# A segment's output projection summed in two PSUM banks (384 and 128 columns), and residual rows assembled once with their batched part

## The chip, the cores and the metric

One core of a Trainium2 chip. The metric is the device time of one execution in microseconds (us); lower is better. The kernel before took 1000.96 us (median of 3 runs, 999.44 to 1001.57). Executions of one kernel agree within about 0.5%.

## The reference

A transformer block with memory, followed by a gMLP. Only the first part matters for this change. The 2048 rows are cut into 64 segments of 32 rows. Each segment is joined with 8 memory rows, goes through attention with 32 heads, and the first 8 output rows are the memory of the next segment. So the segments are a serial chain.

```python
for s in range(n_seg):                       # 64 segments
    xs = x[:, s*seg_len:(s+1)*seg_len, :]    # 32 rows
    h = concatenate([mem, xs], axis=1)       # 40 rows
    q, k, v = h @ Wq, h @ Wk, h @ Wv         # 32 heads of 128
    p = softmax(where(mask, q k^T * scale, -1e9))
    o = (p @ v) @ Wo                         # output projection
    mem = o[:, :M, :]                        # 8 memory rows: the next segment needs them
    outs.append(o[:, M:, :])                 # 32 residual rows
# then h = x + outs, h2 = h + gMLP(layernorm(h)): "the tail" below
```

## The kernel before

An emitter records every operation with the tokens that it reads and writes, and derives the semaphore waits; each engine then runs its own list in program order. This is how waits are put in front of an instruction:

```python
for d in op.waits:                 # one wait for each engine or DMA that is still owed
    if d.is_dma: eng.wait_ge(dma_sems[d.dma_sem], d.dma_val)
    else:        eng.wait_ge(sems[d.eng], d.sigval)
ins = op.fn(eng)
```

PSUM, the memory that TensorE writes its sums to, is declared as 8 banks of 512 float32 columns (`ps`). The parts that the change touches (cut):

```python
def PV_half(s, b):                        # value products of one half of the heads
    for g in range(4):
        for c in range(4): ...            # matmul(ps[:, PVB[c], ...], lhsT=V_sb, rhs=E_sb[..., main columns])
            # reads ("V", b), ("E", b); PVB = (0, 1, 6, 7)
    for c in range(4): ...                # matmul(..., lhsT=Vx, rhs=E_sb[..., extra columns])
            # reads ("Vx", xb), ("E", b); Vx comes by DMA

def Wo(cs, first, last):                  # output projection: 8 matmuls for each c, four at a time (32 columns of the array each)
    for k, c in enumerate(cs):
        for bg in range(8): ...           # matmul(ps[32*g:32*g+32, OB, :], lhsT=cTh[...], rhs=w_o[:, h, :])   512 columns, bank OB
def part_evac(s):                         # ScalarE copies bank OB to SBUF
    act(... out=part[:, s % 4, :], in_=ps[:, OB, :] ...)
def mem_out(s):                           # 16 small matmuls pick and transpose the memory rows, ScalarE copies them to hT
    ...

# one segment, in TensorE's order (cut)
for b in range(2):
    for mi in range(2): QK(s, b, mi); QK_evac(s, b, mi)
S_half(s, 0); sm_exp(0); V_half(s, 0); V_evac(0, "dve"); sm_sums(0); sm_ln(0)
S_half(s, 1); sm_exp(1); sm_rcp(0); V_half(s, 1, (0, 1)); sm_sums(1); sm_ln(1); sm_rcp(1); V_half(s, 1, (2, 3))
V_evac(1, "act"); sm_norm(0); sm_norm(1)
ev = gx.pour(16)                          # 16 filler matmuls, work for a later chunk of 16 segments
PV_half(s, 0); PV_half(s, 1); ...         # then four cT evacuations
if rb > 0: WoX_mm(rb - 1, j4)             # batched part of the rows of four earlier segments
Wo((0, 2), True, False); Wo((1, 3), False, True)
cTx_copy(s); part_evac(s)
late = gv.pour(VXN[i16])                  # fillers: units of 4 matmuls; VXN = 2 in segments 0-11, 4 in 12 and 13, of 16
if j4 == 2: xT(0, XB) ...                 # 4 transposes in every fourth segment; likewise in number 13
mem_out(s)
for f in late: f()                        # ScalarE copies of the fillers (Vs)
if rb > 0 and j4 == 3: WoX_evac(rb - 1)   # ScalarE copy to partx
if j4 == 3:                               # every fourth segment
    F_group(rb, XB); F_add(rb, XB)        # residual rows of the last four segments
    if rb >= 1: WoX_scatter(rb - 1, WXB); h_done(rb - 1, WXB)   # and the batched part, read from partx
```

## Time and profile before

| what | value | view |
|---|---|---|
| span of the profiled execution | 997.6 us | page |
| first segment's first matmul, last segment's first matmul | 55.92, 804.53 us | timeline |
| from one segment's first matmul to the next's, plain segment | 11.64 us | timeline |
| the same for every fourth segment from number 7 on | 12.84 us; 12.33 to 12.36 in six of the fourteen | timeline |
| numbers 13 and 29 | 12.06 us | timeline |
| tail, from the last segment's first matmul to the end | 193.1 us | timeline |

Segments are counted from 0. "Plain" means: no residual work and no collision of fillers.

The windows view gives, for a stretch of time, the busy time of each engine, the clock that TensorE was granted, and the DMA share. In the segments TensorE is busy 93% of the time, at full clock, yet the time is set by a chain of waits:

```profile
core 0: us, PE busy (x) PEld busy (x) DVE busy (x) ACT busy (x) POOL busy (x), PEclk, DMA share, GB/s
400.00:600.00 200.00, 185.68 (x4749) 93.49 (x4744) 100.07 (x236) 118.45 (x271) 21.42 (x51) 1.00 0.19 47
815.00:997.00 182.00, 173.41 (x846) 78.96 (x851) 83.77 (x150) 36.85 (x64) 16.48 (x36) 1.00 0.26 78
```

The timeline lists instructions by start time: start, duration, engine, line, operation, output and inputs, shapes, count, and in brackets how long the engine idled before it and who ended that. Here is the end of a segment of the kernel before (TensorE and ScalarE lines that matter):

```profile
505.46 1.91 PE L581 MATMUL f_ps<-f_arena,f_cT 128*32 128x512 bf16 x32
...
507.20 0.60 PE L401 MATMUL f_ps<-f_arena,f_hTe 128*32 128x512 bf16 x8
507.43 0.60 ACT L593 ACTIVATE f_part<-f_ps 128x512 bf16<-128x512 f32 x1 [1.69 <-PE f_ps L581]
...
508.08 0.27 PE L599 MATMUL f_ps<-f_G_sb,f_part 128*32 128x8 bf16 x16 [0.27 <-ACT f_part L593]
...
508.42 0.20 ACT L602 ACTIVATE f_hT<-f_ps 128x32 bf16<-128x32 f32 x1 [0.40 <-PE f_ps L599]
...
508.67 0.61 PE L438 MATMUL f_ps<-f_arena,f_hT 128*32 128x512 bf16 x8 [0.33 <-ACT f_hT L602]
```

The projection (L581) starts at 505.46, and its last result comes at 507.37. Only then can ScalarE copy all 512 columns (L593, 0.60 us), the memory rows be picked (L599), copied (L602), and the next segment begin (L438) at 508.67: 3.21 us after the start of the projection, of which TensorE fills 0.43 us with two units of fillers (L401).

Every fourth segment ends so:

```profile
148.72 0.60 ACT L593 ACTIVATE f_part<-f_ps 128x512 bf16<-128x512 f32 x1 [1.69 <-PE f_ps L581]
...
149.37 0.27 PE L599 MATMUL f_ps<-f_G_sb,f_part 128*32 128x8 bf16 x16 [0.27 <-ACT f_part L593]
...
149.48 0.39 PE L608 MATMUL f_ps<-f_part,f_F_sb 128*32 128x512 bf16 x4
...
149.80 0.59 ACT L408 ACTIVATE f_Vs<-f_ps 128x512 bf16<-128x512 f32 x1
...
150.28 0.61 ACT L628 ACTIVATE f_partx<-f_ps 128x512 bf16<-128x512 f32 x1
...
150.94 0.40 PE L633 MATMUL f_ps<-f_partx,f_Sc 128*32 128x512 bf16 x4 [1.07 <-ACT f_partx L628]
...
151.16 1.04 PE L438 MATMUL f_ps<-f_arena,f_hT 128*32 128x512 bf16 x16
```

The copy of the batched part (L628, partx) is queued on ScalarE behind the fillers' copy (L408). TensorE's next instruction in order, the scatter (L633), waits 1.07 us for it, and the next segment's first matmul (L438) stands behind the scatter, although it needs nothing from it.

### The profile page before, as it was taken

The page shows a single profiled execution, that of the slowest core. Times are in us where ns is not written, and L with a number is a line of the kernel's source. Part 1 is how long each engine was busy: PE and PEld are TensorE (multiplying, and loading weights), DVE is VectorE, ACT ScalarE, POOL GpSimd, SP SyncE. Part 2 cuts the span into 40 slices and gives each one's busy share as a digit, 9 for nine tenths or more (in the row PEclk, how much of TensorE's full clock was granted, in tenths as well). Part 3 has the DMA queues.
Part 4 walks back from the last instruction along what each step waited for, and adds up shares of the span by engine and source line. Part 5 has one row for each costly group of instructions (what it writes and reads, how often), then busy time and mean ns, then how long its engine had stood idle before and what let it go on. Part 6 is the DMA issues. An engine that isn't in the chain of part 4 may idle for free.

```text
span 997.6 us, 41195 instructions
## 1 busy us (share of the span) xinstructions
PE 891.6 (89%) x18918; PEld 441.2 (44%) x18925; DVE 465.8 (47%) x1045; ACT 489.2 (49%) x1094; POOL 107.9 (11%) x276
## 2 busy tenths in 40 slices
PE   5688998999999999989999999888888889989998
PEld 4434444444444444444444444333333334434443
DVE  3134445455455555554545454545444445454343
ACT  2145555565556555555565666555555565510000
POOL 4000011010111111111111111111011012200000
PEclk9889999999999999999999999999999999999999
DMA  9931112221221111112212121403030167011201
GB/s 334 368 83 35 45 34 56 43 62 41 57 42 55 53 52 49 50 48 35 56 35 55 35 61 37 113 14 95 5 80 12 55 164 229 1 56 52 100 16 34
DMA packets 103651, 71.02 MB, mean 71 GB/s; under 512 B 62248, under 2 KB 89008, under 8 KB 103472
## 3 DMA queue, kind: packets, MB, share of 16 engines
q1 hardware_dynamic: 103472, 68.32, 24.1%
q8 instruction: 150, 2.46, 1.0%
q14 instruction: 29, 0.24, 0.1%
HBM read 39.46 MB, written 18.61 MB: 58 GB/s over the span
## 4 chain that ended last, share of the span: by engine, by line
PE 81%; ACT 12%; SPq 2%; issue 2%; DMA 1%; DVE 1%; POOL 0%; ACTq 0%
PE f_ps L438 23%; PE f_ps L581 12%; PE f_ps L935 10%; PE f_ps L532 8%; PE f_ps L382 6%; PE f_ps L623 3%; ACT f_part L593 3%; PE f_ps L498 3%; ACT f_E_sb L491 3%; ACT f_R_sb L510 2%; PE f_ps L897 2%; PE f_ps L928 2%; PE f_ps L1008 2%; PE f_ps L549 2%; PE f_ps L599 2%
## 5 line engine op out<-in xcount | busy, mean ns | idle before, releaser
L438 PE MATMUL f_ps<-f_arena,f_hT 128*32 128x512 bf16 x4096 | 233.5, 381 | 15.8 <-ACT f_hT L602 15.7
L445 ACT ACTIVATE f_Tst<-f_ps 128x512 bf16<-128x512 f32 x256 | 152.8, 597 | 113.0 <-PE f_ps L438 113.0
L438 PEld LDWEIGHTS f_ps<-f_arena,f_hT 128*32 128x32 bf16 x4096 | 105.3, 97 | 120.8 <-ACT f_hT L602 20.6
L532 PE MATMUL f_ps<-f_arena,f_hT 128*32 128x512 bf16 x2048 | 143.6, 378 | 0.0
L451 DVE STREAM_TRANSPOSE f_QT<-f_Tst 128x256 uint32<-128x256 uint32 x128 | 56.5, 442 | 183.5 <-ACT f_Tst L445 183.5
L581 PE MATMUL f_ps<-f_arena,f_cT 128*32 128x512 bf16 x2048 | 122.3, 380 | 2.3 <-ACT f_cT L568 2.2
L935 PE MATMUL f_ps<-f_arena 128*128 128x512 bf16 x448 | 101.3, 379 | 2.4 <-DVE f_arena L941 1.6
L593 ACT ACTIVATE f_part<-f_ps 128x512 bf16<-128x512 f32 x64 | 38.2, 597 | 108.0 <-PE f_ps L581 108.0
L454 DVE STREAM_TRANSPOSE f_KT<-f_Tst 128x256 uint32<-128x256 uint32 x128 | 57.0, 445 | 53.1 <-ACT f_Tst L445 53.1
L581 PEld LDWEIGHTS f_ps<-f_arena,f_cT 128*32 128x32 bf16 x2048 | 48.8, 96 | 74.0 <-ACT f_cT L568 32.2
L461 POOL COPY f_QT<-f_arena 128x256 bf16<-128x256 bf16 x64 | 29.8, 465 | 397.3 <-PE f_ps L483 397.2
L570 DVE TENSOR_SCALAR f_cT<-f_ps 128x320 bf16<-128x320 f32 x128 | 56.9, 487 | 33.1 <-PE f_ps L555 33.1
L382 PEld LDWEIGHTS f_ps<-f_hTe,f_arena 128*128 128x128 bf16 x1024 | 61.1, 102 | 20.5 <-issue 20.4
L382 PE MATMUL f_ps<-f_hTe,f_arena 128*128 128x128 bf16 x1024 | 69.7, 226 | 0.0
L935 PEld LDWEIGHTS f_ps<-f_arena 128*128 128x128 bf16 x448 | 43.5, 98 | 55.9 <-DVE f_arena L941 2.6
L568 ACT ACTIVATE f_cT<-f_ps 128x320 bf16<-128x320 f32 x128 | 49.0, 434 | 37.2 <-PE f_ps L555 37.2
L518 DVE SCALAR_TENSOR_TENSOR f_E_sb<-f_R_sb,f_E_sb 128x160 bf16<-128x160 f32 x128 | 41.7, 326 | 54.5 <-ACT f_R_sb L514 54.5
L491 ACT ACTIVATE f_E_sb<-f_ps,f_shift 128x224 bf16<-128x224 f32 x128 | 56.9, 444 | 0.0
L514 ACT ACTIVATE f_R_sb<-f_R_sb,f_rbias 128x160 f32<-128x160 f32 x128 | 54.0, 422 | 2.1
L510 ACT ACTIVATE f_R_sb<-f_ps 128x160 f32<-128x160 f32 x128 | 38.8, 303 | 29.9 <-PE f_ps L503 25.0
L589 POOL COPY f_cTx<-f_cT 128x256 bf16<-128x256 bf16 x64 | 26.1, 408 | 212.5 <-DVE f_cT L570 212.5
L401 PE MATMUL f_ps<-f_arena,f_hTe 128*32 128x512 bf16 x512 | 38.6, 411 | 9.1 <-ACT f_Vs L408 9.1
(97 smaller groups left out, 1042.7 us busy)
## 6 DMA issues: line engine op xcount, KB each, us to landing
wT_d<-f_wst SPq DMA_DIRECT2D x32, 256.0 KB, 2.3
f_arena<-wT_d SPq DMA_DIRECT2D x32, 256.0 KB, 4.6
f_arena<-in_A_Wq_dram SPq DMA_DIRECT2D x4, 1024.0 KB, 9.0
f_arena<-in_A_Wk_dram SPq DMA_DIRECT2D x4, 1024.0 KB, 13.9
f_arena<-in_A_Wv_dram SPq DMA_DIRECT2D x4, 1024.0 KB, 11.5
f_arena<-in_A_Wo_dram SPq DMA_DIRECT2D x4, 1024.0 KB, 13.6
vext_d<-f_Vs SPq DMA_DIRECT2D x32, 128.0 KB, 2.0
f_Vx<-vext_d SPq DMA_DIRECT2D x64, 64.0 KB, 2.4
```

What stands on the lines that cost most here:

```text
L382: pe(lambda e, h=h, dc=dc, hh=hh: e.matmul(ps[:, bank, hh * 128:(hh + 1) * 128], lhsT=ws[:, dc, h * DH:(h + 1) * DH], rhs=hTe[:, ck % 2, d ...
L438: pe(lambda e, dc=dc, c=c, rhs=rhs: e.matmul(ps[32 * c:32 * c + 32, bank, :], lhsT=hT[:, sl, dc, :], rhs=rhs, start=(dc == 0), stop=(dc == ...
L445: act(lambda e: e.activation(out=Tst[:, tb, :].rearrange("p (hp i r) -> p hp i r", i=32, r=2), in_=ps[:, bank, :].rearrange("p (hp r i) -> ...
L451: dve(lambda e: e.transpose(out=dst, in_=src), reads=[("T", tb)], writes=[("QT", b)])
L454: dve(lambda e: e.transpose(out=dst, in_=src), reads=[("T", tb)], writes=[("KT", b)])
L491: act(lambda e: e.activation(out=E_sb[:, b, :], in_=ps[:, bank, 0:224], func=ACT.Exp, scale=scale, bias=shift_sb[:, 0:1]), reads=[PB(bank) ...
L510: act(lambda e: e.activation(out=R_sb[:, b, :], in_=ps[:, bank, 224:384], func=ACT.Ln, scale=LNS), reads=[PB(bank)], writes=[("R", b)])
L532: pe(lambda e, dc=dc, c=c, c0=c0: e.matmul(ps[32 * c:32 * c + 32, bank, :], lhsT=hT[:, sl, dc, :], rhs=w_v[:, dc, c0:c0 + 512], start=(dc ...
L570: dve(lambda e: e.tensor_scalar(out=dst, in0=src, scalar1=UNSC, scalar2=None, op0=ALU.mult), reads=[PB(PVB[c])], writes=[("cT", c)])
L581: pe(lambda e, h=h, g=g, i=i, k=k, b=b: e.matmul(ps[32 * g:32 * g + 32, OB, :], lhsT=cTh[:, i, 8:40], rhs=w_o[:, h, :], start=(first and k ...
L593: act(lambda e: e.activation(out=part[:, s % 4, :], in_=ps[:, OB, :], func=ACT.Copy), reads=[PB(OB)], writes=[("part", s % 4)])
L935: pe(lambda e: e.matmul(ps[:, bank, 0:TB], lhsT=z2[:, sc, fb * 128:(fb + 1) * 128], rhs=wTb[tb % 2][:, :, sc, :], start=(sc == 0), stop=(s ...
```

## The change

The intent: copy the first 384 columns of the projection while TensorE still sums the other 128 in another bank, so that only a short copy remains before the memory rows; and put the residual rows together once, in one bank with their batched part, without a wait in front of the next segment. The fillers are placed anew, the second V product is issued as 12 and 4 matmuls instead of 8 and 8, and the extra columns of E get a token of their own. The core of the diff (cut):

```diff
-    GB = 7
+    GB = 1
+    OB2 = 0
+    OC = 384
     def sm_exp(b):
-            reads=[PB(bank), "shift"], writes=[("E", b)])
+            reads=[PB(bank), "shift"], writes=[("E", b), ("Ex", b)])
     # sm_sums, sm_norm, PV_half: the operations on the extra columns
-                reads=[("Vx", xb), ("E", b)], writes=[PB(PVB[c])])
+                reads=[("Vx", xb), ("Ex", b)], writes=[PB(PVB[c])])
-    def Wo(cs, first, last):
+    def Wo(cs, bank, d0, d1):                  # columns d0 to d1 into the given bank
-    def part_evac(s):
+    def part_evac(s, bank, d0, d1):
-                   reads=[("part", s % 4), "G"], writes=[PB(GB)])
+                   reads=[("part", s % 8, dc // 3), "G"], writes=[PB(GB)])
     def F_group(rb, bank):
-            ... rhs=part[:, j, :], start=True, stop=True
+            ... rhs=part[:, i, :], start=True, stop=False      # i = (4 * rb + j) % 8
     def WoX_scatter(rb, bank):
-            ... rhs=partx[:], start=True, stop=True
+            ... rhs=partx[:], start=False, stop=True           # adds to F_group's bank
-    VXN = [2] * 12 + [4, 4, 0, 0]
+    VXS = (0, 1, 4, 5, 7, 8, 9, 12)
-        V_half(s, 1, (0, 1))
+        V_half(s, 1, (0, 1, 2))
...
-        V_half(s, 1, (2, 3))
+        V_half(s, 1, (3,))
         if rb > 0:
             WoX_mm(rb - 1, j4)
-        Wo((0, 2), True, False)
-        Wo((1, 3), False, True)
+            if j4 == 3:
+                WoX_evac(rb - 1)
+        vx = i16 in VXS
+        late = gv.pour(vx)                                     # one unit ahead of the projection
+        Wo((0, 2, 1, 3), OB, 0, OC)
+        part_evac(s, OB, 0, OC)
+        Wo((0, 2, 1, 3), OB2, OC, D)
         cTx_copy(s)
-        part_evac(s)
+        part_evac(s, OB2, OC, D)
+        if j4 == 3 and rb > 0:
+            F_group(rb - 1, XB)
+            WoX_scatter(rb - 1, XB)
+            h_done(rb - 1, XB)
-        late = gv.pour(VXN[i16])
+        late += gv.pour(2 * vx)                                # two after it
         if s + 1 < NSEG:
             mem_out(s)
+        late += gv.pour(vx)                                    # one after the memory rows
-        if rb > 0 and j4 == 3:
-            WoX_evac(rb - 1)
-        if j4 == 3 and s + 1 < NSEG:
-            F_group(rb, XB)
-            F_add(rb, XB)
-            if rb >= 1:
-                WoX_scatter(rb - 1, WXB)
-                h_done(rb - 1, WXB)
```

More of the change, by code (lines that the diff above doesn't have):

```diff
@@ L218, in fast_path @@
     cT = sb("cT", [128, 4, 320], BF)
-    part = sb("part", [128, 4, 512], BF)
+    part = sb("part", [128, 8, 512], BF)
     partx = sb("partx", [128, 512], BF)
     xn = sb("xn", [128, 2, 512], BF)
-    hbuf = sb("hbuf", [128, 4, 512], BF)
+    hbuf = sb("hbuf", [128, 2, 512], BF)
     xo = sb("xo", [128, 2, 512], BF)
@@ L232, in fast_path @@
     m0 = sb("m0", [M, D], BF)
-    stats = sb("stats", [128, RB, 2, 6], F32)
+    stats = sb("stats", [128, 2, 6], F32)
     mv = sb("mv", [128, RB, 2], F32)
@@ L505, in sm_sums @@
                                             skip_group_check=True, tile_position=(0, 32 * c)),
-               reads=[("E", b), "ones"], writes=[PB(bank)])
+               reads=[("Ex", b), "ones"], writes=[PB(bank)])
     def sm_ln(b):
@@ L523, in sm_norm @@
         dve(lambda e: e.scalar_tensor_tensor(out=ev, in0=rv, scalar=RK, in1=ev, op0=ALU.mult, op1=ALU.mult),
-            reads=[("R", b), ("E", b)], writes=[("E", b)])
+            reads=[("R", b), ("Ex", b)], writes=[("Ex", b)])
     def V_half(s, b, dcs=range(DC)):
@@ L573, in fast_path @@
     cTh = cT[:].rearrange("p c (b g q) -> p (c b g) q", b=2, q=40)
-    def Wo(cs, first, last):
-        for k, c in enumerate(cs):
+    def Wo(cs, bank, d0, d1):
+        for c in cs:
             for bg in range(8):
@@ L580, in Wo @@
                 i = 8 * c + bg
-                pe(lambda e, h=h, g=g, i=i, k=k, b=b: e.matmul(
-                    ps[32 * g:32 * g + 32, OB, :], lhsT=cTh[:, i, 8:40], rhs=w_o[:, h, :], start=(first and k == 0 and b == 0),
-                    stop=(last and k == len(cs) - 1 and b == 1), tile_position=(0, 32 * g)),
-                    reads=[("cT", c), ("Wo", h // 8)], writes=[PB(OB)])
+                pe(lambda e, h=h, g=g, i=i, b=b, c=c: e.matmul(
+                    ps[32 * g:32 * g + 32, bank, 0:d1 - d0], lhsT=cTh[:, i, 8:40], rhs=w_o[:, h, d0:d1], start=(c == 0 and b == 0),
+                    stop=(c == 3 and b == 1), tile_position=(0, 32 * g)),
+                    reads=[("cT", c), ("Wo", h // 8)], writes=[PB(bank)])
     def cTx_copy(s):
@@ L590, in cTx_copy @@
              writes=[("cTx", (s // 4) % 2)])
-    def part_evac(s):
-        act(lambda e: e.activation(out=part[:, s % 4, :], in_=ps[:, OB, :], func=ACT.Copy), reads=[PB(OB)], writes=[("part", s % 4)])
+    def part_evac(s, bank, d0, d1):
+        act(lambda e: e.activation(out=part[:, s % 8, d0:d1], in_=ps[:, bank, 0:d1 - d0], func=ACT.Copy), reads=[PB(bank)],
+            writes=[("part", s % 8, d0 // OC)])
     def mem_out(s):
@@ L598, in mem_out @@
                 c0 = dc * 128 + 32 * c
-                pe(lambda e, dc=dc, c=c, c0=c0: e.matmul(ps[32 * c:32 * c + 32, GB, dc * M:(dc + 1) * M], lhsT=part[:, s % 4, c0:c0 + 32],
+                pe(lambda e, dc=dc, c=c, c0=c0: e.matmul(ps[32 * c:32 * c + 32, GB, dc * M:(dc + 1) * M], lhsT=part[:, s % 8, c0:c0 + 32],
                                                          rhs=G_sb[:, :], start=True, stop=True, skip_group_check=True, tile_position=(0, 32 * c)),
-                   reads=[("part", s % 4), "G"], writes=[PB(GB)])
+                   reads=[("part", s % 8, dc // 3), "G"], writes=[PB(GB)])
         act(lambda e: e.activation(out=hT[:, slot(s + 1), :, 0:M], in_=ps[:, GB, 0:DC * M].rearrange("p (dc c) -> p dc c", c=M), func=ACT.Copy),
@@ L607, in F_group @@
         for j in range(4):
-            pe(lambda e, j=j: e.matmul(ps[32 * j:32 * j + 32, bank, :], lhsT=F_sb[:, :], rhs=part[:, j, :], start=True, stop=True,
-                                       tile_position=(0, 32 * j)),
-               reads=[("part", j), "F"], writes=[PB(bank)])
+            i = (4 * rb + j) % 8
+            pe(lambda e, i=i, j=j: e.matmul(ps[32 * j:32 * j + 32, bank, :], lhsT=F_sb[:, :], rhs=part[:, i, :], start=True, stop=False,
+                                            tile_position=(0, 32 * j)),
+               reads=[("part", i, 0), ("part", i, 1), "F"], writes=[PB(bank)])
     def F_add(rb, bank):
-        dve(lambda e: e.tensor_tensor(out=hbuf[:, rb % 4, :], in0=ps[:, bank, :], in1=hbuf[:, rb % 4, :], op=ALU.add),
-            reads=[PB(bank), ("h", rb % 4)], writes=[("h", rb % 4)])
+        dve(lambda e: e.tensor_tensor(out=hbuf[:, rb % 2, :], in0=ps[:, bank, :], in1=hbuf[:, rb % 2, :], op=ALU.add),
+            reads=[PB(bank), ("h", rb % 2)], writes=[("h", rb % 2)])
     def load_h(rb):
-        sp(lambda e: e.dma_start(hbuf[:, rb % 4, :], xr[:, rb, :]), writes=[("h", rb % 4)])
+        sp(lambda e: e.dma_start(hbuf[:, rb % 2, :], xr[:, rb, :]), writes=[("h", rb % 2)])
     def WoX_mm(rb, qr):
@@ L632, in WoX_scatter @@
             q = slice(32 * c, 32 * c + 32)
-            pe(lambda e, q=q, c=c: e.matmul(ps[q, bank, :], lhsT=Sc[:, q], rhs=partx[:], start=True, stop=True, tile_position=(0, 32 * c)),
+            pe(lambda e, q=q, c=c: e.matmul(ps[q, bank, :], lhsT=Sc[:, q], rhs=partx[:], start=False, stop=True, tile_position=(0, 32 * c)),
                reads=["partx", "Sc"], writes=[PB(bank)])
@@ L637, in h_done @@
         F_add(rb, bank)
-        dve(lambda e: e.bn_stats(out=stats[:, rb, 0, :], in_=hbuf[:, rb % 4, :]), reads=[("h", rb % 4)], writes=[("st", rb)])
-        dve(lambda e: e.bn_aggr(out=mv[:, rb, :], in_=stats[:, rb, 0, :]), reads=[("st", rb)], writes=[("mv", rb)])
+        dve(lambda e: e.bn_stats(out=stats[:, rb % 2, :], in_=hbuf[:, rb % 2, :]), reads=[("h", rb % 2)], writes=[("st", rb % 2)])
+        dve(lambda e: e.bn_aggr(out=mv[:, rb, :], in_=stats[:, rb % 2, :]), reads=[("st", rb % 2)], writes=[("mv", rb)])
         pool(lambda e: e.tensor_scalar(out=rstd[:, rb:rb + 1], in0=mv[:, rb, 1:2], scalar1=EPS, scalar2=None, op0=ALU.add),
@@ L643, in h_done @@
              reads=[("rstd", rb), "mhalf"], writes=[("rstd", rb)])
-        sp(lambda e: e.dma_start(h_d[rb], hbuf[:, rb % 4, :]), reads=[("h", rb % 4)], writes=[("hd", rb)])
+        sp(lambda e: e.dma_start(h_d[rb], hbuf[:, rb % 2, :]), reads=[("h", rb % 2)], writes=[("hd", rb)])
     def xn2_apply(rb, j):
-        dve(lambda e: e.tensor_scalar(out=xo[:, j, :], in0=hbuf[:, rb % 4, :], scalar1=mv[:, rb, 0:1], scalar2=rstd[:, rb:rb + 1],
+        dve(lambda e: e.tensor_scalar(out=xo[:, j, :], in0=hbuf[:, rb % 2, :], scalar1=mv[:, rb, 0:1], scalar2=rstd[:, rb:rb + 1],
                                       op0=ALU.subtract, op1=ALU.mult),
-            reads=[("h", rb % 4), ("mv", rb), ("rstd", rb)], writes=[("xo", j)])
+            reads=[("h", rb % 2), ("mv", rb), ("rstd", rb)], writes=[("xo", j)])
     def xn2_store(rb, j):
@@ L710, in fast_path @@
         load_vx(s)
-    load_h(0)
     class Gap:
@@ L773, in fast_path @@
             qkx_atoms(ck, i16)
-        if j4 == 0 and rb + 1 < RB:
-            load_h(rb + 1)
+        if j4 == 1 and rb > 0:
+            load_h(rb - 1)
+        if s == NSEG - 1:
+            load_h(rb)
         if s % 2 == 0 and s // 2 < NWT:
@@ L958, in fast_path @@
         if rb == 0:
-            WoX_scatter(RB - 2, 1)
             F_group(RB - 1, XB)
-            h_done(RB - 2, 1)
-            F_add(RB - 1, XB)
         z2_mm(rb, 1, zbank())
@@ L971, in fast_path @@
         if rb == 1:
-            WoX_scatter(RB - 1, 1)
-            h_done(RB - 1, 1)
+            WoX_scatter(RB - 1, XB)
+            h_done(RB - 1, XB)
             for r in range(RB):
```

## The prediction

> **What bounds it.** The timeline shows 64 serial segments from 56 to 816 us, then a dense tail of about 180 us (TensorE 173 of 182 us busy in the windows view). The clock was granted in full there (1.00), DMA 19%. Segments start 11.64 us apart; after every fourth (from the eighth on) it is 12.84, about 12.33 in the last quarter. Each segment needs the previous one's memory rows, so its chain of waits is the bound, not TensorE's work: the last sixteen segments lack 16 filler matmuls (0.9 us) and still take 11.61.
>
> The end of a segment, from the start t0 of the output projection (32 matmuls, four at a time): t0+1.91 they end, +1.97 ScalarE copies 512 columns (0.60), +2.62 16 small matmuls, +2.96 ScalarE copy (0.20), +3.21 the next segment's first matmul. TensorE has 1.3 us after its last projection matmul in which only 0.43 us of filler runs. At every fourth segment the partx copy (0.61) queues behind the memory-row copy and often a Vs copy; TensorE waits 1.07 us for it, in order, before it may start the next segment.
>
> **The change.**
> 1. Split into 384 and 128 columns. The streams stay about 1.73 us (1.30 + 0.44; the 40-column matmuls in the trace start 6 ns apart, so 64 weight loads should keep up). Copies fitted from 320 columns (434 ns) and 512 (597 ns): 0.49 and 0.27, estimates. The fit's slope, 0.85 ns a column, agrees with "ScalarE: Activation LUTs", Rules for kernel authors (about 0.83 ns an element). First copy from t0+1.55 to 2.04; second from 1.99 (it waits for its matmuls) to 2.26; only four small matmuls remain after it: next segment at about t0+2.82. Gain 0.39 us x 63 = 24 us. Separate banks are needed: "PSUM — Partial Sum Buffer", PSUM bank collisions, forbids TensorE writing a bank which ScalarE reads; the trace before shows only the serialised form.
> 2. Residual rows: the partx copy moves ahead of the projection, where ScalarE idles 1.69 us. F_group and scatter add up in one bank, 0.43 us of TensorE in the gap. One of two VectorE adds goes. The excess of every fourth segment vanishes: 11 x 1.20 + 3 x 0.7 = 15 us, and about 0.5 at the start of the tail. The seventh-numbered segment of sixteen has fillers too and may lose 0.3, three times.
> 3. Filler moves: one unit (0.21 us) before the projection, where TensorE idles 0.18 after WoX: 0 to 0.03 us, about -0.5 in total.
> 4. V split 12+4 and the separate token for extra columns: nearly nothing (1 us). The value products wait for the second V copy on ScalarE (their third matmul writes the bank it reads); that copy queues behind the exponentials, not behind V or the normalisation.
>
> Sum: 24 + 15 + 0.5 + 1 - 1.5 = 39, nearly all on the critical path. The tail stays.
>
> **Time: 961 us, 8 in 10 between 952 and 971.** Faster by over 2%: 0.97; within 2%: 0.03; slower: 0.
>
> **Signs.** Segments 11.2 to 11.3 us apart, every fourth the same within 0.2 but for numbers 7, 23, 39. part copies of about 490 and 270 ns, the second starting 0.4 us after the first. TensorE's wait for the partx copy gone in the loop. Value products still released by the V copy. Tail within 1 us of before.
>
> **What would make it wrong.** The 128-column matmuls bound by weight loads: the second copy starts later, gain halves. ScalarE not overlapping the two copies: 0.05 to 0.1 us less each. The fuller TensorE losing clock. Filler in front of the projection or before the small matmuls colliding: period up in the eight filler segments of sixteen only. Shorter segments exposing the transposes' DMA or the load of w_in1 at the tail's start.

## The result

The changed kernel took 968.75 us (967.63 to 969.03, 4 runs), and the kernel before, in the same session, 1000.21 us (999.44 to 1001.57, 4 runs). The ratio is 0.9682, with a 95% interval of 0.9665 to 0.9699. Here and below a ratio is the mean time of one kernel's fast runs over the mean of the other's of the same rounds, so it is not quite the ratio of the medians. The time lies inside the stated range; the gain of 31.5 us is 7.5 us short of the 39 forecast.

The profile after has a span of 965.9 us. Its last segment starts at 771.21, its first at 55.93:

| what | before | after |
|---|---|---|
| first to last segment | 748.6 us | 715.3 us |
| plain segment | 11.64 | 11.27 (11.30 to 11.31 with fillers) |
| every fourth | 12.84 or 12.33 | 11.28 to 11.31; numbers 7, 23, 39: 11.73, 11.72, 11.78 |
| isolated long segments | number 34: 11.76 | numbers 5, 9, 20, 24, 49: 11.44 to 11.86 |
| tail | 193.1 us | 194.7 us |

(The expectations below say 11.28 for the changed kernel's plain segment; the unrounded starts give 11.27.) So the loop gained 33.3 us and the tail lost 1.6. The end of a segment with fillers now:

```profile
485.17 1.92 PE L584 MATMUL f_ps<-f_arena,f_cT 128*32 128x384 bf16 x64
...
486.70 0.72 ACT L596 ACTIVATE f_part<-f_ps 128x384 bf16<-128x384 f32 x2 [1.29 <-PE f_ps L584]
...
486.92 0.60 PE L401 MATMUL f_ps<-f_arena,f_hTe 128*32 128x512 bf16 x8
...
487.35 0.31 PE L603 MATMUL f_ps<-f_G_sb,f_part 128*32 128x8 bf16 x16
...
487.51 0.39 PE L401 MATMUL f_ps<-f_arena,f_hTe 128*32 128x512 bf16 x4
487.71 0.20 ACT L606 ACTIVATE f_hT<-f_ps 128x32 bf16<-128x32 f32 x1 [0.29 <-PE f_ps L603]
...
487.96 1.26 PE L440 MATMUL f_ps<-f_arena,f_hT 128*32 128x512 bf16 x20
```

The projection (L584) starts at 485.17 and ends at 487.09, as long as before (1.92 us). The two copies (L596) start at 486.70, while it still runs, and the next segment starts at 487.96: 2.79 us after the projection's start instead of 3.21. The trace shows no wait for ScalarE reading one bank while TensorE writes another, and the results were correct, as "PSUM — Partial Sum Buffer", PSUM bank collisions, of the Trainium skill states for different banks. The two copies by shape, from the groups of instructions (count, busy time, mean ns):

```profile
L596 ACT ACTIVATE f_part<-f_ps 128x384 bf16<-128x384 f32 x64 | 31.4, 490 | 73.9 <-PE f_ps L584 73.9
L596 ACT ACTIVATE f_part<-f_ps 128x128 bf16<-128x128 f32 x64 | 17.7, 277 | 0.0
```

They take 490 and 277 ns; the estimates were 490 and 270. Every fourth segment (here number 11):

```profile
190.40 0.61 ACT L633 ACTIVATE f_partx<-f_ps 128x512 bf16<-128x512 f32 x1
...
191.77 0.72 ACT L596 ACTIVATE f_part<-f_ps 128x384 bf16<-128x384 f32 x2 [0.77 <-PE f_ps L584]
...
191.99 0.39 PE L613 MATMUL f_ps<-f_part,f_F_sb 128*32 128x512 bf16 x4
...
192.21 0.39 PE L638 MATMUL f_ps<-f_partx,f_Sc 128*32 128x512 bf16 x4
...
192.42 0.31 PE L603 MATMUL f_ps<-f_G_sb,f_part 128*32 128x8 bf16 x16
...
193.06 1.26 PE L440 MATMUL f_ps<-f_arena,f_hT 128*32 128x512 bf16 x20 [0.32 <-ACT f_hT L606]
```

The partx copy (L633) runs during the projection, and the scatter (L638) follows without an idle time before it. That part works as forecast too. What is missing lies elsewhere. First, the value products. Before, from the second V copy on (lines L539, L549, L555, L568):

```profile
503.81 0.58 ACT L539 ACTIVATE f_V_sb<-f_ps 128x512 bf16<-128x512 f32 x1
...
504.45 0.27 PE L549 MATMUL f_ps<-f_E_sb,f_V_sb 32*128 32x40 bf16 x16
...
504.56 0.19 PE L555 MATMUL f_ps<-f_E_sb,f_Vx 32*128 32x64 bf16 x4
...
504.98 0.77 ACT L568 ACTIVATE f_cT<-f_ps 128x320 bf16<-128x320 f32 x2 [0.59 <-PE f_ps L555]
```

and after, the same instructions (now L541, L551, L557, L570):

```profile
483.44 0.58 ACT L541 ACTIVATE f_V_sb<-f_ps 128x512 bf16<-128x512 f32 x1
...
483.86 0.48 PE L551 MATMUL f_ps<-f_E_sb,f_V_sb 32*128 32x40 bf16 x16
...
484.24 0.21 PE L557 MATMUL f_ps<-f_E_sb,f_Vx 32*128 32x64 bf16 x4
...
484.64 0.77 ACT L570 ACTIVATE f_cT<-f_ps 128x320 bf16<-128x320 f32 x2 [0.62 <-PE f_ps L557]
```

Before, the V copy ends at 504.39 and the first cT evacuation starts at 504.98, 0.59 us later. After, it ends at 484.02, and the evacuation starts at 484.64, 0.62 us later, although TensorE had come early enough to issue the first products before the copy ended. From the first value product (L551) to the first product on the extra columns (L557) it is now 0.38 us.

Second, TensorE's clock in the tail. After (windows; the column after POOL's busy time is the granted clock):

```profile
core 0: us, PE busy (x) PEld busy (x) DVE busy (x) ACT busy (x) POOL busy (x), PEclk, DMA share, GB/s
...
862.00:865.00 3.00, 3.00 (x9) 1.08 (x8) 0.00 (x0) 0.00 (x0) 0.00 (x0) 0.50 0.92 296
```

For 3.4 us the clock was half. It follows the check for non-finite values, for which TensorE idles in both kernels:

```profile
860.55 0.16 PE L894 MATMUL f_ps<-f_onesrc,f_okb 128*1 128x1 bf16 x1 [1.80 <-DVE f_okb L893]
```

```profile
893.97 0.16 PE L886 MATMUL f_ps<-f_onesrc,f_okb 128*1 128x1 bf16 x1 [1.80 <-DVE f_okb L885]
```

In the trace of before the same idle time of 1.80 us is there, and no lowered clock follows it (windows, columns as above; see e7):

```profile
895.30:898.70 3.40, 3.40 (x17) 1.53 (x16) 0.65 (x1) 0.00 (x0) 0.00 (x0) 1.00 1.00 325
```

### The profile page after: what moved, and what is told of

Same layout as the page of the kernel before. It is cut to its first block, busy times and chain, and to the rows that moved or that the text cites. A ratio compares the mean times of both kernels' runs of the same rounds, so it can differ in the third digit from the quotient of the medians.

```text
span 965.9 us, 45422 instructions
## 1 busy us (share of the span) xinstructions
PE 899.0 (93%) x20966; PEld 492.4 (51%) x20973; DVE 445.2 (46%) x1029; ACT 499.9 (52%) x1158; POOL 108.3 (11%) x276
## 3 DMA queue, kind: packets, MB, share of 16 engines
q1 hardware_dynamic: 103472, 68.32, 25.2%
## 4 chain that ended last, share of the span: by engine, by line
PE 88%; ACT 4%; DMA 3%; SPq 2%; issue 2%; DVE 1%; POOL 0%; ACTq 0%
PE f_ps L440 24%; PE f_ps L584 12%; PE f_ps L534 11%; PE f_ps L943 10%; PE f_ps L382 5%; PE f_ps L628 4%; PE f_ps L551 3%; PE f_ps L500 3%; PE f_ps L905 3%; PE f_ps L936 2%; PE f_ps L1013 2%; PE f_ps L401 2%; PE f_ps L603 2%; SPq L707 2%; ACT f_hT L606 1%
## 5 line engine op out<-in xcount | busy, mean ns | idle before, releaser
L440 PEld LDWEIGHTS f_ps<-f_arena,f_hT 128*32 128x32 bf16 x4096 | 103.7, 97 | 122.4 <-ACT f_hT L606 24.2
L534 PE MATMUL f_ps<-f_arena,f_hT 128*32 128x512 bf16 x2048 | 143.9, 378 | 0.3 <-issue 0.3
L584 PE MATMUL f_ps<-f_arena,f_cT 128*32 128x384 bf16 (+1 forms) x4096 | 123.3, 273 | 1.7 <-ACT f_cT L570 1.5
L584 PEld LDWEIGHTS f_ps<-f_arena,f_cT 128*32 128x32 bf16 x4096 | 84.7, 97 | 55.8 <-ACT f_cT L570 27.5
L596 ACT ACTIVATE f_part<-f_ps 128x384 bf16<-128x384 f32 (+1 forms) x128 | 46.3, 384 | 73.9 <-PE f_ps L584 73.9
L570 ACT ACTIVATE f_cT<-f_ps 128x320 bf16<-128x320 f32 x128 | 49.0, 435 | 40.9 <-PE f_ps L557 40.9
L551 PE MATMUL f_ps<-f_E_sb,f_V_sb 32*128 32x40 bf16 x2048 | 43.3, 177 | 15.8 <-ACT f_V_sb L541 12.1
L534 PEld LDWEIGHTS f_ps<-f_arena,f_hT 128*32 128x32 bf16 x2048 | 44.3, 95 | 22.0 <-issue 0.7
```

Of the source, the lines that this page charges most:

```text
L440: pe(lambda e, dc=dc, c=c, rhs=rhs: e.matmul(ps[32 * c:32 * c + 32, bank, :], lhsT=hT[:, sl, dc, :], rhs=rhs, start=(dc == 0), stop=(dc == ...
L534: pe(lambda e, dc=dc, c=c, c0=c0: e.matmul(ps[32 * c:32 * c + 32, bank, :], lhsT=hT[:, sl, dc, :], rhs=w_v[:, dc, c0:c0 + 512], start=(dc ...
L551: pe(lambda e, q=q, c=c, g=g, c0=c0: e.matmul(ps[:, PVB[c], c0:c0 + 40], lhsT=V_sb[q, b, g * 128:(g + 1) * 128], rhs=E_sb[q, b, g * 40:(g ...
L584: pe(lambda e, h=h, g=g, i=i, b=b, c=c: e.matmul(ps[32 * g:32 * g + 32, bank, 0:d1 - d0], lhsT=cTh[:, i, 8:40], rhs=w_o[:, h, d0:d1], star ...
```

## The experiments

Theories. A: split and residual rows give what was forecast, and the missing 7.5 us are separate small losses: a second wait on one matmul that the new token brings, isolated idle times that the trace puts down to nothing but issue, and the half clock in the tail. The rivals: the split itself is dearer than thought (e1), the residual part is (e2), or the new V order makes TensorE stall (e3, e4).

### e1: the split alone

The kernel before with the two-bank projection and nothing else.

```diff
-        Wo((0, 2), True, False)
-        Wo((1, 3), False, True)
-        part_evac(s)
+        Wo((0, 2, 1, 3), OB, 0, OC)
+        part_evac(s, OB, 0, OC)
+        Wo((0, 2, 1, 3), OB2, OC, D)
+        part_evac(s, OB2, OC, D)      # and two tokens of part, GB = 1, OB2 = 0
```

> Before plus the two-bank projection alone. Theory A (the split itself gains what was forecast, and the missing time is lost elsewhere): plain segments 11.23 us apart (before 11.64, the changed kernel 11.28), every fourth still 1.2 us longer, about 975 us. Rival B (64 narrower matmuls and two copies are themselves dearer than forecast): 11.28 us or more, about 979 us.

980.50 us against 999.77 (ratio 0.9808, 0.9793 to 0.9823). Plain segments are 11.24 us apart: the split gives 0.40 us a segment, as forecast (0.39), and rival B is out. Every fourth is 12.44, still 1.2 longer. The total missed the expected 975, because segments with a transpose rose to 11.65, number 12 to 11.65 as well: with the shorter hole, fillers and transposes no longer fit into it (see e5). The half clock in the tail (194.9 us, before 193.1) is in this trace too.

### e2: the residual part alone

The changed kernel with the projection in one bank, V 8+8, one token, fillers as before.

```diff
-        Wo((0, 2, 1, 3), OB, 0, OC) ... Wo((0, 2, 1, 3), OB2, OC, D) ... part_evac(s, OB2, OC, D)
+        Wo((0, 2, 1, 3), OB, 0, D)
+        part_evac(s, OB, 0, D)
```

> The changed kernel with the projection in one bank again, V 8+8, one token and the fillers as before: only the residual part is left. Theory A: plain segments 11.64 us apart, the excess of every fourth gone (13.9 us in the loop), about 986 us. Rival B (the residual part costs something in every segment, or the scatter still waits): plain segments above 11.66 or every fourth above 11.9.

985.33 us against 999.77 (ratio 0.9865, 0.9850 to 0.9880). Plain segments 11.64, every fourth 11.64 too (numbers 13 and 29 stay at 12.06). Theory A holds. The gain in the loop is the sum of the excesses of before, 8 x 1.20 + 6 x 0.71 = 13.9 us. Numbers 18, 22, 32 and 34 are at 11.70 to 11.75, so isolated longer segments occur without the split as well. The tail is 193.1 us (983.1 minus 790.05) as before: the 0.5 us forecast at its start did not come.

### e3: one token

```diff
-            reads=[PB(bank), "shift"], writes=[("E", b), ("Ex", b)])
+            reads=[PB(bank), "shift"], writes=[("E", b)])      # and ("E", b) wherever ("Ex", b) was read
```

> The changed kernel with one token for both column groups of E. Theory A: in the changed kernel the matmul on the extra columns carries two waits (a DMA and VectorE), and the second wait holds TensorE's sequencer some 0.06 us in a place where it is not ahead; with one token that gap goes and plain segments fall from 11.28 to 11.22 us, 3.5 us in all (about 965). Rival B: the gap is due to the V split (TensorE comes early and stalls at the bank wait); then 11.28 us stays, 968.7.

962.55 us against 999.77 (ratio 0.9628, 0.9615 to 0.9641), where the changed kernel has 0.9682: 5 us faster without the part of the change that was to let the products start sooner. Plain segments are 11.22 us apart, 0.05 less: 3.2 us in all, where 3.5 were forecast. The rest is that the five isolated long segments are gone in this trace (numbers 5, 9, 20, 24 and 49 at 11.22 to 11.26; but 1 and 6 are at 11.47 and 11.41).

### e4: V 8+8

```diff
-        V_half(s, 1, (0, 1, 2)) ... V_half(s, 1, (3,))
+        V_half(s, 1, (0, 1)) ... V_half(s, 1, (2, 3))
```

> The changed kernel with the second V product split 8+8 again. Theory A: nothing but 0 to 0.03 us a segment lost (V copy queues behind the exponentials), 968.7 to 970.5 us, and the 0.07 us gap ahead of the extra columns stays. Rival B (the split of V causes the gap): segments fall to about 11.22 us and 965 us.

967.18 us (ratio 0.9676, 0.9662 to 0.9689; the changed kernel has 0.9682, 0.9665 to 0.9699): the same. Plain segments stay at 11.28. The V order is neither the cause of the loss nor a gain; rival B is out.

### e5: the fillers where they were

```diff
-        vx = i16 in VXS
-        late = gv.pour(vx)            # before Wo
-        late += gv.pour(2 * vx)       # after Wo
-        late += gv.pour(vx)           # after mem_out
+        late = gv.pour(VXN[i16])      # after Wo, VXN = [2] * 12 + [4, 4, 0, 0]
```

> The changed kernel with the fillers where the kernel before had them (two units after the projection in twelve segments, four in two). Theory A: the shortened hole after the projection no longer holds fillers and a transpose or the residual matmuls, so the filler move is what lets the split pay: segments with a transpose at 11.69 us, those with residual matmuls at about 11.7, numbers 12 and 13 up to 12.1, all others 11.28; about 8 to 10 us slower than the changed kernel, 977 us. Rival B (the forecast: the filler move is worth 0 to 0.5 us either way): 968 us.

974.87 us against 999.71 (ratio 0.9746, 0.9732 to 0.9761): about 6 us slower than the changed kernel. Segments with a transpose take 11.69 to 11.71 us, those with residual matmuls 11.70 to 11.75, numbers 13 and 29 12.12. The size was expected a little larger, the pattern is right. A segment with fillers and a transpose:

```profile
271.70 1.93 PE L584 MATMUL f_ps<-f_arena,f_cT 128*32 128x384 bf16 x64
...
273.45 0.61 PE L401 MATMUL f_ps<-f_arena,f_hTe 128*32 128x512 bf16 x8
...
273.99 0.40 PE L348 MATMUL f_ps<-f_ident,f_xn 128*128 128x128 bf16 x4
...
274.32 0.27 PE L603 MATMUL f_ps<-f_G_sb,f_part 128*32 128x8 bf16 x16
...
274.91 0.83 PE L440 MATMUL f_ps<-f_arena,f_hT 128*32 128x512 bf16 x12 [0.32 <-ACT f_hT L606]
```

After the projection (L584, from 271.70) come fillers (L401), transposes (L348) and only then, 2.62 us after the projection's start, the memory-row matmuls (L603), which in the changed kernel start 2.18 us after it (487.35 less 485.17, above). The fillers stream for 0.43 us from 273.45, that is to 273.88; the transposes, which use the whole width of the array, start at 273.99, and four of them (about 0.06 us each) are streamed by 274.22, but the next matmuls start at 274.32. So each change between four-at-a-time and full-width matmuls costs about 0.1 us. Without such a change there is no gap: in the changed kernel the fillers stream for 0.43 us from 486.92, and the memory-row matmuls, four at a time as well, start at 487.35. "TensorEngine Tiling (Array Packing)", Tiling Modes, Key Properties, of the Trainium skill states that a change of tiling mode drains TensorE; this trace agrees: it has a gap at each change and gives its size.

### e6: one token, and the filler group of segment 7 moved to 13

```diff
-    VXS = (0, 1, 4, 5, 7, 8, 9, 12)
+    VXS = (0, 1, 4, 5, 8, 9, 12, 13)
```

> One token as in e3, and the filler group of segment 7 of sixteen moved to 13. Theory A: the 11.68 us of segments 7, 23 and 39 fall to 11.24, and 13, 29 and 45 rise by 0.1 at most: 1 us better than e3, about 961.5. Rival B (segment 7 is long for the residual matmuls alone): no change.

962.48 us against 999.71 (ratio 0.9624, 0.9611 to 0.9637): no better than e3. Numbers 7, 23 and 39 did fall to 11.24, but 13 and 29 rose to 11.66, by 0.4 and not 0.1: number 13 has transposes too in two of the chunks, with the two mode changes of e5, which the expectation had left out. Number 45, without transposes, is at 11.25.

### e7: the check's matmul later

e6, with the matmul of the finite check issued after two more groups of the tail.

```diff
+            if tb == 1 and fb == 1:
+                check2()              # the PE matmul and the flag, formerly part of check()
```

> e6 with the one matmul of the finite check issued after two more groups of the tail, so that TensorE does not idle 1.8 us for it. Theory A: the half clock window of 3.4 us that the tail of the changed kernel shows follows that idle time; without it no tail window has a lowered clock, and the tail (from the last segment's start to the end) falls from 194.7 us to 191.3 (1.8 idle, 1.6 clock), against 193.1 before. Rival B (the clock dips at random, or for another reason): the tail falls by 1.8 us only and dips stay.

958.76 us against 999.71 (ratio 0.9589, 0.9576 to 0.9602), 3.7 us less than e6 in the same session. The tail is 190.8 us (957.3 minus 766.49), against 195.2 in e6. In this stretch of the trace, where the idle time was, TensorE is busy throughout and the clock stays at 1.00 (windows, columns as above):

```profile
853.00:856.00 3.00, 3.00 (x16) 1.35 (x15) 1.64 (x4) 0.00 (x0) 0.00 (x0) 1.00 0.29 100
856.00:859.00 3.00, 3.00 (x16) 1.35 (x14) 1.38 (x2) 0.00 (x0) 0.00 (x0) 1.00 0.99 324
```

The idle time is needed for the dip: e7, e8 and e12, which do not have it, have no dip. It is not sufficient. Of the eleven traces with that idle time, eight have a half clock window of 3.4 us right behind it: the changed kernel (both traces) and e1, e3, e4, e5, e6, e9. Three have none: before, e2 and e11. They are the ones without the split, but the traces point to something else. In each trace all changes of the clock lie whole multiples of 3.41 us apart, so the trace can be laid out in windows of that length. The 1.80 us of idle time and the 0.26 us that follow 0.16 us later fall into these windows differently in each execution. In the eight traces one window holds 1.88 to 2.06 us of idle time, and the half clock is the next window. In the other three no window holds more than 1.81 us, because an edge cuts the idle time (before: 1.80 us between 890.64 and 894.06, 0.26 in the next). So the dip went with where the windows lay in that execution, which is chance as far as the traces show, and not with the split. This was read from the traces afterwards; no run tests it. The times fit: of the 27 runs of before in the three sessions of experiments, the seven of 1000.6 us and more have a mean clock of 0.988 to 0.990, the others 0.989 to 0.991, but these runs left no trace.

### e8: no filler ahead of the projection

e7, with units 0, 2, 2 instead of 1, 2, 1 (before the projection, after it, after the memory rows).

```diff
-        late = gv.pour(vx)
+        late = []
-        late += gv.pour(vx)
+        late += gv.pour(2 * vx)
```

> e7 with no filler ahead of the projection, two units after it and two after the memory-row matmuls. Theory A: the unit ahead of the projection costs the 0.03 us by which filler segments are longer (11.25 against 11.22); behind the memory rows two units of 0.43 us fit in the wait of 0.4 us: filler segments 11.22 to 11.26, 0 to 0.7 us gained. Rival B: the two units delay the next segment, 11.3 us or more in filler segments.

957.43 us against 999.71 (ratio 0.9573, 0.9560 to 0.9586), 1.3 us below e7, with overlapping intervals. The trace decides it: segments with fillers fell from 11.25 to 11.22 us, like those without. Two units do fit behind the memory rows.

### e9: the second wait moved

The changed kernel, both tokens kept. The wait for the DMA that brings Vx is put on the second V product. (Its first matmul, L534, which takes the wait, starts at 482.59 in this run's trace, 2.5 us before L557 at 485.09; the expectation says 0.9.)

```diff
-                   reads=[("hTx", ...), ("hTm", s), ("W", 2, 2 * b), ("W", 2, 2 * b + 1)], writes=[PB(bank)])
+                   reads=[("hTx", ...), ("hTm", s), ("W", 2, 2 * b), ("W", 2, 2 * b + 1)] + [("Vx", s % NVX)] * b, writes=[PB(bank)])
```

> The changed kernel, its two tokens kept; the wait for the Vx load is put on the second V product, 0.9 us earlier, where it holds nothing up. The matmul on the extra columns then has the VectorE wait alone. Theory A (two waits on one matmul cost the gap): the gap of 0.07 us goes, plain segments 11.22 to 11.24 us, about 964 us. Rival B (any wait on the late VectorE operation costs it, or the token itself): 11.28 us stays, 968.

TensorE's instruction streams show what was changed. The matmul on the extra columns of the first half waits (the number of the DMA semaphore differs from segment to segment)

```
before:           L555  [fdma7]            (DMA)
changed kernel:   L557  [fdma37, fs_dve]   (DMA and VectorE)
e9:               L557  [fs_dve]           (VectorE)
```

964.47 us against 999.08 (ratio 0.9641, 0.9624 to 0.9659), where the changed kernel, in the same session (e10), has 967.74. Plain segments 11.22 us. (The first segment of the profiled run took 15.61 us, 11.6 to 12.6 in the other traces; this is its slowest run, and what held it was not looked into.) The value products:

```profile
484.36 0.58 ACT L541 ACTIVATE f_V_sb<-f_ps 128x512 bf16<-128x512 f32 x1
...
484.79 0.48 PE L551 MATMUL f_ps<-f_E_sb,f_V_sb 32*128 32x40 bf16 x16
...
485.09 0.20 PE L557 MATMUL f_ps<-f_E_sb,f_Vx 32*128 32x64 bf16 x4
...
485.51 0.77 ACT L570 ACTIVATE f_cT<-f_ps 128x320 bf16<-128x320 f32 x2 [0.56 <-PE f_ps L557]
```

From L551 to L557 it is 0.30 us, not 0.38, and the evacuation starts 0.57 us after the V copy's end (484.94), not 0.62. The same token and the same VectorE operation are waited for; only the number of waits on that matmul is different. So the loss of 0.06 us at the evacuation, 0.05 in the distance of segments, is due to two waits on one instruction. The packed trace shows how. It keeps a record that the timeline leaves out: in the changed kernel, e4, e5 and e10, an EVENT_SEMAPHORE instruction of TensorE's queue, 0.051 us long, stands ahead of the first product on the extra columns in all of the 63 segments looked at (484.14 to 484.19 beside the lines of the changed kernel shown above, where L557 starts at 484.24). No trace of another run has it there. The second wait is an instruction of its own. Elsewhere a second wait is hidden: in 48 segments the first score matmul of the first half (L477 before) carries two, of GpSimd and VectorE, and starts 0.10 us after the matmuls ahead of it all the same, like that of the second half, which carries one. Its EVENT_SEMAPHORE instruction is done 1.1 to 1.3 us before the matmul starts: there TensorE's queue is ahead.

### e10: the changed kernel once more

> The changed kernel once more, beside the others. If the isolated long segments (numbers 5, 9, 20, 24, 49) come from where instruction fetches fall in the program they come again at the same numbers; if from chance they move. The half clock window in the tail: again, if it is a matter of this kernel's timing.

967.74 us against 999.08 (ratio 0.9680, 0.9662 to 0.9698). The isolated long segments came again at the same numbers: 5 (11.67), 9 (11.35), 20 (11.39), 24 (12.01) and 49 (11.70). The clock was half at the same place of the tail. So the long segments belong to the program, not to chance. In number 24 of the first trace:

```profile
340.08 0.31 PE L603 MATMUL f_ps<-f_G_sb,f_part 128*32 128x8 bf16 x15
340.72 0.18 PE L603 MATMUL f_ps<-f_G_sb,f_part 128*32 128x8 bf16 x1 [0.33 <-issue]
```

TensorE stops for 0.33 us in the middle of 16 equal small matmuls, and the trace names no releaser ("issue").

### e11: more instructions in the kernel before

```diff
+        if j4 != 2 and i16 not in (12, 13):
+            for k in range(40): ...   # matmul(ps[.., XB, 0:8], lhsT=ident, rhs=G_sb), read by nothing
```

> The kernel before with 40 further matmuls of 8 columns, into a bank nothing reads, in the idle time ahead of the memory-row matmuls of 36 of the 64 segments: 1440 matmuls and as many weight loads. Theory A (more instructions make fetches fall late now and then): plain segments 11.64 us as before, but a few isolated ones 0.1 to 0.6 us longer, 1 to 2 us in all. Rival B: no isolated ones; the time stays within 0.3 us of before.

998.81 us against 999.08 (ratio 0.9987, 0.9971 to 1.0004). No isolated long segments worth the name (one of 11.68 among 11.60). Theory A falls: the number of instructions alone does not bring them. They are fewer where the second wait is gone (e3, e6 to e8, e9), but e9 still has 11.50 and 11.41 at numbers 5 and 6. Their cause stays open. One trail: the ten stops of TensorE over 0.15 us that the loops of all traces put down to issue (after, e4, e5, e9 and e10, numbers 5, 20, 24 and 49) all come 1.2 to 1.5 us after the end of a packet of the DMA queue that carries instructions (kind "instruction"). That points to late fetches of instructions; no run tests it, and most packets are followed by no stop.

### e12: all that helped

e7 with two filler units after the memory rows in segments 0 to 13, and two more after the projection in 0 and 1 only.

```diff
+        late = gv.pour(2 * (i16 < 2))      # after the projection
+        late += gv.pour(2 * (i16 < 14))    # after mem_out
```

> e7 with the fillers spread: two units after the memory-row matmuls of segments 0 to 13 of sixteen, two more after the projection in 0 and 1 only. From the experiments so far: every segment 11.22 to 11.26 us, also numbers 13 and 29; loop about 708 us, tail 191; 956 to 957 us.

956.55 us against 999.08 (ratio 0.9569, 0.9555 to 0.9583). All segments after the first take 11.21 to 11.24 us but two (11.27 and 11.31). This version beats both kernels: 43 us below before, 11 below the changed kernel of the same session.

## Why the prediction was right or wrong

The time, the direction and the main mechanism were right. The sum by terms, in us (the loop's terms from the distances of segments; a loss is negative):

| term | forecast | measured | by |
|---|---|---|---|
| 1. split | 24 | 25.2 (0.40 x 63) | e1 |
| 2. residual rows, loop | 15 | 13.9 | e2 |
| 2. residual rows, start of the tail | 0.5 | 0 | e2 |
| 3. fillers: segments with fillers | -0.5 | -0.6 (0.03 x 21) | trace after, e8 |
| 3. fillers: numbers 7, 23, 39 | -1 | -1.3 (0.44 x 3) | trace after, e6 |
| 3. fillers: collision of 13 and 29 gone | not seen | +0.8 (0.42 x 2) | both traces |
| 4. V split and token | +1 | -3.2 (0.05 x 63) | e3, e4, e9 |
| isolated long segments | not seen | -1.7 | trace after, e10 |
| half clock in the tail, in the traced execution | not seen | -1.6 | trace after, e7 |
| sum | 39 | 31.5 | profiles: 31.7 |

Point by point:

- "t0+1.55 to 2.04; second from 1.99 ... to 2.26 ... next segment at about t0+2.82": measured from the trace, the first copy starts at t0+1.53, both are done by 2.25, and the next segment starts at t0+2.79. "The 128-column matmuls bound by weight loads" did not happen: 64 matmuls take as long as the 32 before (1.92 and 1.91 us).
- "The excess of every fourth segment vanishes: 11 x 1.20 + 3 x 0.7": it vanishes. The count was off: it was 8 x 1.20 and 6 x 0.71, for three segments of the first eleven (numbers 15, 31, 47) have no fillers' copy in ScalarE's queue.
- "Filler moves: ... 0 to 0.03 us": right for the direct cost. But their worth was missed. Without the move the shorter hole does not hold what the longer one did, and 6 us of the split's gain are lost (e5).
- "V split 12+4 and the separate token for extra columns: nearly nothing (1 us)". This is the step that failed. The V split is nothing (e4), and the reason given, the V copy behind the exponentials on ScalarE, stands: after as before, TensorE waits for the V copy (in the waits view of after, 12.1 us in the sixteen segments without other matmuls ahead of the value products). But the token is a loss of 3.2 us. Finer tokens mean more waits, and the argument counted only what a wait waits for, not that one more wait on the same matmul is one more instruction of 0.05 us on the chain. e3 and e9 show it.
- "Tail within 1 us of before": wrong by 0.6, for the half clock window, and the traces put that down to where the windows of the clock lay, that is to luck, and not to the change (e7). "The fuller TensorE losing clock" named the clock as a risk, but in the wrong place: the loop stayed at 1.00, and it was an idle time of the tail, which the kernel before has too, that cost it.

Open are the isolated long segments (1.7 us). That the half clock depends on where the windows lie is read from the traces, not tested.

## What to carry to other kernels

Cut the last accumulation of a serial chain so that most of its evacuation runs while the rest is still being summed; then look at what had been living in the hole that has become shorter, for moving it can be worth a quarter of the gain. Count waits per instruction when refining dependencies: a second semaphore on one matmul, just after the engine has been released, is one more instruction in its queue (0.05 us here) and costs more than the earlier start can give if that start was not what the chain waited for. A copy that TensorE needs should be queued on ScalarE before the long wait, not behind it.

## What the Trainium skill lacked or had wrong

- No page states what a second semaphore wait on one TensorE instruction costs. Here it was 0.05 us a segment, an EVENT_SEMAPHORE instruction of 0.051 us ahead of a matmul just after a release (plain segments 11.27 us with it, 11.22 without: e3, e9).
- "TensorE: Matmul & The Clock Gate", HAM oscillation — how this bites in real kernels, gives as the rule that TensorE should have no idle gaps over about 3.4 us. Here an idle time of 1.80 us, followed by one of 0.26, was enough for a half clock window of 3.4 us in eight traces of eleven; in these 1.88 to 2.06 us of it lay in one window, in the other three 1.81 at most; with the idle time removed none came (e7). The page's free-running windows of 3.4 us agree in length.
- The same page, "Wait — 56ns, not 53.3ns?", states that matmuls never start less than about 25 ns apart. That does not hold for matmuls in different column tiles: 16 of 40 columns start within 0.10 us, about 6 ns apart (lines below, L479 to L485); within one column tile they are 25 to 29 ns apart, so there the figure agrees. Part 3 of the page, on packing, has the smaller figure of 4 ns.
- "TensorEngine Tiling (Array Packing)", Key Properties, says that a change of tiling mode drains TensorE, without a figure: about 0.1 us at each change here (e5).
- "ScalarE: Activation LUTs", Rules for kernel authors: the slope of 0.83 ns an element agrees (490 and 277 ns for 384 and 128 columns: 0.83). The fixed part of about 0.3 us, stated for a bias given by pointer, agrees for the exponential with such a bias (422 ns for 160 elements, less 133), and for an ACTIVATE without pointer operands the page states 186 ns + 0.833 ns an element (What ACT_TABLE_LOAD costs). The copies here have a fixed part of 170 ns (277 ns less 128 x 0.83), 16 ns less.

The lines of the changed kernel for the third point:

```profile
491.43 0.27 PE L470 MATMUL f_ps<-f_mask,f_ident 128*32 128x224 bf16 x4
491.52 0.27 PE L479 MATMUL f_ps<-f_QT,f_KT 128*32 128x40 bf16 x16
491.63 0.20 PE L485 MATMUL f_ps<-f_QT,f_arena 128*32 128x64 bf16 x4
```
